# Weight decoding in a fused attention and feed-forward kernel: low parts of the first twelve blocks from TensorE instead of VectorE

## The chip, the core and the metric

The kernel runs on one core of a Trainium2 chip. A core has TensorE (PE, matrix products into PSUM), VectorE (DVE), ScalarE (ACT), GpSimd (POOL) and SyncE (SP, which here issues DMAs). Each engine takes its instructions in the order in which they were placed on it, and waits on semaphores where it needs another engine's result. The metric is the device time of one execution in microseconds (us); lower is better.

## The reference, cut to what matters

```python
B, H, S, D = 4, 8, 768, 64              # q, k, v in float32
scores = matmul(q, k.T) / 8
keep = (pos_k < n_sink) | ((0 <= pos_q - pos_k) & (pos_q - pos_k < window))   # 4 sinks, window 128
a = softmax(where(keep, scores, -1e9))
x = matmul(a, v)                        # -> 3072 rows of 512
h = x @ w_in                            # 512 x 2048
g = where(h >= 1, h, where(h <= -1, 0, (h + 1)**2 / 4))
out = g @ w_out                         # 2048 x 512
```

The weights `w_in` and `w_out` arrive as 8-byte floating-point words (the host passes the memory as pairs of 32-bit integers). The kernel turns them into float32 numbers on the chip, and then splits each into a high part (rounded to the format that TensorE reads in one pass, F32R in the code) and a low part (the rest), since each product of the feed-forward is computed as high*high + high*low + low*high.

## The kernel before, in words

The work is cut into 64 attention units of 3 blocks of 128 query rows: one head of one batch, first or second half of the sequence. Eight units (the eight heads) make a chunk of 384 rows, and there are eight chunks. Unit 0 to 7 are chunk 0, 8 to 15 chunk 1, and so on. A unit is made of: loads of q, k and v (SP); three score products (TensorE, line 239); mask and row maximum (VectorE, line 243); exponential (ScalarE, line 246); one over the sum (GpSimd line 251, VectorE line 252); normalisation (ScalarE line 264 and VectorE line 266 in the first 16 units, which are called native); transposes (TensorE lines 324 and 326), their copies out of PSUM (ScalarE lines 327 and 331); and the product with v (`av2`, line 367 for the native units) with its copy `xn` (line 369). The score products and `av2` of native units take plain float32 operands.

After a chunk's attention comes its feed-forward: `split` (lines 479, 480), 16 `stage1` steps (line 439, products with `w_i`), the activation (446 to 450) and 16 `stage2` steps (line 458, products with `w_o`). TensorE alone is written in program order by hand (`manual_schedule`): the attention steps of one chunk are interleaved with the feed-forward steps of the chunk before by `spread`. The order of all other engines is set when the program is built: a list scheduler, which runs through the program with its own estimate of each duration, places each instruction when it takes it to be ready, earlier program text first. That order is then fixed.

There are 32 weight blocks of 128 x 512 numbers, numbered n = 0 to 31: even n is block n/2 of `w_in` (tile `wi0`, `wi1`, ...), odd n of `w_out` (tile `w`). `weights(n)` loads the raw words (issued by SP for n below 8, by ScalarE after that, `AHEAD` blocks ahead) and calls `decode` (lines 151 to 157): three VectorE instructions put the float32 number together in a tile `o` (lines 153, 154, 155), ScalarE casts it to the high part (156), VectorE subtracts to get the low part (157). The tile `o` has two buffers, so that the first instruction of block n+2 (line 153) needs the last reader of block n's `o` to be done. In program order the first six blocks (`WFIRST`) are spread over the attention of units 0 to 9, when there is no feed-forward yet; the next 22 over units 10 to 17, beside the feed-forward of chunk 0's first half; the last four after that.

## Time and profile before

| | before |
|---|---|
| time, median of 3 runs | 736.66 us (735.27 to 738.84) |
| the profiled execution: its own time | 737.31 us |
| its span, first to last instruction | 735.5 us |
| TensorE busy | 696.8 us, 95% of the span |
| VectorE busy | 528.7 us, 72% |
| ScalarE busy | 507.0 us, 69% |
| GpSimd busy | 307.2 us, 42% |
| mean granted TensorE clock | 0.988 |
| DMA | 77.79 MB, mean 106 GB/s |

The shares are means over stages that differ: the first 150 us hold all weight decoding. The profile cuts the span into 40 slices of 18.4 us, and the trace can be asked for the busy time of each engine in any stretch, for the groups of instructions in it, and for the instructions in order of time. A tile's name in a row stands without its buffer number, and shapes are partitions x elements.

### The profile page before, as it was taken

What the parts mean: (1) busy time and instruction counts of PE and PEld (TensorE: products, weight loads), DVE (VectorE), ACT (ScalarE), POOL (GpSimd) and SP (SyncE); (2) the same over time, 40 slices, a digit from 0 to 9 for tenths busy, and PEclk for the clock granted to TensorE, in tenths of its full rate; (3) what the DMA queues carried; (4) which work ended last, traced back from release to release, by engine and by line L of the source; (5) the groups of instructions that cost most, each with busy time, mean ns of one, the idle gap of its engine ahead of it and who ended that gap; (6) DMA issues with size and microseconds to landing.
All of it is one profiled execution on the core that took longest, in us unless ns stands there. A gap on an engine that the chain in (4) does not pass through costs nothing.

```text
span 735.5 us, 12356 instructions
## 1 busy us (share of the span) xinstructions
PE 696.8 (95%) x3841; PEld 615.7 (84%) x3841; DVE 528.7 (72%) x1396; ACT 507.0 (69%) x1313; POOL 307.2 (42%) x537
## 2 busy tenths in 40 slices
PE   5669889899999999999999999999999999999996
PEld 3337678789999999999979998899889999989995
DVE  8999996987655666568777887877887777742221
ACT  4888797776576665578767876778767776645342
POOL 3112166554346434236554555645666454500000
PEclk9989999999999999999999999999999999999998
DMA  8987543312131311134423542324334342101001
GB/s 268 327 268 255 170 115 96 99 46 54 42 100 45 100 40 58 34 119 128 124 81 117 156 121 85 116 73 156 124 114 119 103 131 85 66 2 44 0 1 47
DMA packets 48265, 77.79 MB, mean 106 GB/s; under 512 B 13632, under 2 KB 32064, under 8 KB 48192
## 3 DMA queue, kind: packets, MB, share of 16 engines
q1 hardware_dynamic: 44736, 64.34, 28.9%
q10 hardware_dynamic: 3456, 12.58, 4.8%
q8 instruction: 32, 0.52, 0.3%
q14 instruction: 41, 0.34, 0.2%
HBM read 69.83 MB, written 7.08 MB: 105 GB/s over the span
## 4 chain that ended last, share of the span: by engine, by line
PE 64%; DVE 17%; ACT 7%; DMA 7%; issue 2%; POOL 2%; SPq 0%; ACTq 0%; POOLq 0%; DVEq 0%
PE o_ps L458 28%; PE h_ps L439 27%; PE ps_a L402 4%; DMA w<-w_in 4%; PE ps_a L239 3%; ACT p L246 2%; DVE p L266 2%; DVE k_s L223 1%; DVE o L154 1%; PE ps_a L334 1%; DVE o L155 1%; DVE p L258 1%; DVE gl L450 1%; DVE p L243 1%; DVE o L153 1%
## 5 line engine op out<-in xcount | busy, mean ns | idle before, releaser
L439 PE MATMUL h_ps<-x,wi 128*128 128x384 f32 x1536 | 308.7, 340 | 0.4 <-DVE x L480 0.4
L439 PEld LDWEIGHTS h_ps<-x,wi 128*128 128x128 f32 x1536 | 263.5, 188 | 9.3 <-DVE x L480 0.7
L458 PE MATMUL o_ps<-w,gh 128*128 128x512 f32 x768 | 244.6, 399 | 0.0
L458 PE MATMUL o_ps<-w,gl 128*128 128x512 f32 x384 | 151.3, 394 | 0.0
L458 PEld LDWEIGHTS o_ps<-w,gh 128*128 128x128 f32 x768 | 135.2, 189 | 15.7 <-issue 0.3
L446 ACT ACTIVATE g<-h_ps,half 128x384 f32<-128x384 f32 x128 | 73.9, 578 | 69.7 <-PE h_ps L439 67.7
L448 DVE SCALAR_TENSOR_TENSOR g<-g,h_ps 128x384 f32<-128x384 f32 x128 | 70.2, 549 | 68.6 <-ACT g L447 68.0
L246 ACT ACTIVATE p<-p,peak 128x260 f32<-128x260 f32 (+1 forms) x192 | 93.9, 489 | 33.9 <-DVE peak L243 32.0
L225 POOL TENSOR_TENSOR q_l<-r,q_h 128x384 fp32r<-128x384 f32 x48 | 50.3, 1047 | 142.5 <-ACT q_h L224 141.6
L449 ACT CAST gh<-g 128x384 fp32r<-128x384 f32 x128 | 65.5, 512 | 56.9 <-DVE g L448 55.9
L243 DVE CUSTOM_DVE_ANT_0 p<-ps_a,m 128x260 f32<-128x260 f32 (+1 forms) x176 | 68.5, 398 | 31.8 <-PE ps_a L239 30.5
L239 PE MATMUL ps_a<-k_s,q_h 128*128 128x260 f32 (+1 forms) x240 | 71.2, 345 | 18.6 <-DMA k_s<-qk 6.1
L458 PEld LDWEIGHTS o_ps<-w,gl 128*128 128x128 f32 x384 | 72.3, 188 | 17.5
L450 DVE TENSOR_TENSOR gl<-g,gh 128x384 fp32r<-128x384 f32 x112 | 68.0, 607 | 24.5 <-ACT gh L449 23.6
L223 DVE TENSOR_TENSOR k_s<-k_r,k_s 64x524 fp32r<-64x524 f32 (+1 forms) x44 | 45.4, 1032 | 40.9 <-ACT k_s L221 40.9
L239 PEld LDWEIGHTS ps_a<-k_s,q_h 128*128 128x128 f32 x240 | 45.2, 203 | 33.3 <-issue 10.9
L447 ACT ACTIVATE g<-g 128x384 f32<-128x384 f32 x128 | 67.0, 523 | 2.7
L346 POOL TENSOR_SCALAR_AFFINE_SELECT pt<-pt 128x384 fp32r<-128x384 f32 (+1 forms) x96 | 50.8, 530 | 24.2 <-DVE pt L339 21.7
L266 DVE TENSOR_SCALAR p<-p,stat 128x132 f32<-128x132 f32 (+1 forms) x160 | 59.1, 418 | 0.3
L344 POOL TENSOR_SCALAR_AFFINE_SELECT pt<-pt 128x384 fp32r<-128x384 f32 (+1 forms) x96 | 52.5, 547 | 8.9 <-ACT pt L338 3.9
L251 POOL TENSOR_SCALAR stat<-stat 128x3 f32<-128x3 f32 x64 | 28.6, 447 | 62.2 <-ACT p L246 53.8
L402 PEld LDWEIGHTS ps_a<-pt,v_s 128*128 128x128 f32 x304 | 46.5, 189 | 2.0
(117 smaller groups left out, 955.3 us busy)
## 6 DMA issues: line engine op xcount, KB each, us to landing
r<-qk SPq DMA_DIRECT2D x48, 192.0 KB
k_r<-qk SPq DMA_DIRECT2D x32, 262.0 KB
again<-w_in SPq DMA_DIRECT2D x16, 512.0 KB
again<-w_out SPq DMA_DIRECT2D x16, 512.0 KB
w<-w_in ACTq DMA_DIRECT2D x12, 512.0 KB
w<-w_out ACTq DMA_DIRECT2D x12, 512.0 KB
out<-o SPq DMA_DIRECT2D x23, 256.0 KB
r<-vx SPq DMA_DIRECT2D x32, 128.0 KB
```

Of the source, the lines that this page charges most:

```text
L239: nc.tensor.matmul(ps[:, lo:260], lhsT=q[:, i * P:(i + 1) * P], rhs=k_s[:, c0:c0 + 260 - lo], start=(j == 0), stop=(j == len(qs) - 1))
L243: nc.vector.tensor_tensor_reduce(out=p[:, i, lo:260], in0=ps[:, lo:260], in1=m, scale=-0.0625 if units.index(u) < NATIVE else -0.125, scal ...
L246: nc.scalar.activation(p[:, i, lo:260], p[:, i, lo:260], AF.Exp, bias=peak_i, scale=-1.0, accum_out=stat[:, i:i + 1])
L266: (nc.gpsimd if eng == "p" else nc.vector).tensor_scalar(p[:, i, lo:260], p[:, i, lo:260], r, None, op0=ALU.mult)
L402: nc.tensor.matmul(z, lhsT=w, rhs=y, start=(n == 0), stop=(n == len(mms) - 1))
L439: nc.tensor.matmul(h_ps[:, :T], lhsT=w_i[j][:, w, ct * P:(ct + 1) * P], rhs=x[:, y, ct], start=(ct == 0 and n == 0), stop=(ct == NCT - 1 a ...
L446: nc.scalar.activation(g, h_ps[:, :T], AF.Relu, bias=half, scale=0.5)
L447: nc.scalar.activation(g, g, AF.Square)
L448: nc.vector.scalar_tensor_tensor(g, g, 1.0, h_ps[:, :T], op0=ALU.min, op1=ALU.max)
L449: nc.scalar.copy(gh, g)
L450: (nc.gpsimd if row0 == GL_POOL else nc.vector).tensor_tensor(gl, g, gh.bitcast(F32), op=ALU.subtract)
L458: nc.tensor.matmul(o_ps[tt], lhsT=gg[:, tt * P:(tt + 1) * P], rhs=w_o[j][:, w], start=(j == js[0] and n == 0), stop=(j == js[-1] and n == 2))
```

## The change

For blocks 0 to 11 the subtraction on VectorE is left out. Two matrix products take its place: identity times the float32 number `o` (plain float32 operands), and minus identity times the high part (F32R operands), added up in one PSUM tile of the pool `ps_o`; ScalarE copies this out into the low part. `weights(n)` calls this (`lows`) for block n-1 after it has decoded block n. `neg` is minus the identity. `WFIRST` goes from 6 to 12, so that blocks 0 to 11 are spread over units 0 to 9, and blocks 12 to 27 over units 10 to 17. Blocks 12 to 31 are decoded as before, the subtraction now on line 158. All lines behind it have numbers that are 19 higher than before (243 becomes 262, 324 becomes 343).

```diff
-WFIRST = 6
+WFIRST = 12
...
-    def decode(t, w, words):
+    def decode(t, w, words, lo=True):
         low, x = words[:, :, 0], words[:, :, 1]
         nc.vector.tensor_scalar(w, x, 3, 0x3FFFFFFF, op0=ALU.logical_shift_left, op1=ALU.bitwise_and)
         nc.vector.scalar_tensor_tensor(w, x, -0x40000000, w, op0=ALU.bitwise_and, op1=ALU.bitwise_or)
         nc.vector.scalar_tensor_tensor(w, low, 29, w, op0=ALU.logical_shift_right, op1=ALU.bitwise_or)
         nc.scalar.copy(t[:, 0], w.bitcast(F32))
-        nc.vector.tensor_tensor(t[:, 1], w.bitcast(F32), t[:, 0].bitcast(F32), op=ALU.subtract)
+        if lo:
+            nc.vector.tensor_tensor(t[:, 1], w.bitcast(F32), t[:, 0].bitcast(F32), op=ALU.subtract)
+
+
+    neg = const.tile([P, P], F32R, name="neg")
+    nc.vector.tensor_scalar(neg, ident, -1.0, None, op0=ALU.mult)
+    todo = {}
+
+    def lows(n):
+        if n not in todo:
+            return
+        t, w = todo.pop(n)
+        ps = ps_o.tile([P, DM], F32, name="o_ps")
+        nc.tensor.matmul(ps, lhsT=ident, rhs=w.bitcast(F32), start=True, stop=False)
+        nc.tensor.matmul(ps, lhsT=neg, rhs=t[:, 0], start=False, stop=True)
+        nc.scalar.copy(t[:, 1], ps)
...
-            decode((w_i, w_o)[i][j], moe.tile([P, DM], I32, name="o"), words)
+            t, w = (w_i, w_o)[i][j], moe.tile([P, DM], I32, name="o")
+            decode(t, w, words, n >= WFIRST)
+            lows(n - 1)
+            if n < WFIRST:
+                todo[n] = t, w
```

How this moves instructions shows best at three places. The first is VectorE where unit 10 begins, the first unit that runs beside the feed-forward. `p_651` (before) and `p_736` (changed) are the score tile of unit 10, `o_...` the number of a block, `wi8` the low and high part of block 16, `wi6` that of block 12. Before:

```order
L157 TENSOR_TENSOR w_1006<-o_1007,w_1006 128x512
L154 SCALAR_TENSOR_TENSOR o_1022<-w_915,o_1022 128x512
L153 TENSOR_SCALAR o_1057<-w_968 128x512
L155 SCALAR_TENSOR_TENSOR o_1022<-w_915,o_1022 128x512
L154 SCALAR_TENSOR_TENSOR o_1057<-w_968,o_1057 128x512
L243 ISA p_651,peak_97<-ps_a_653,m0_109 128x128
L243 ISA peak_97 128x1
L243 ISA p_651,peak_97<-ps_a_665,m1n_108 128x260
L243 ISA peak_97 128x1
L155 SCALAR_TENSOR_TENSOR o_1057<-w_968,o_1057 128x512
L157 TENSOR_TENSOR wi8_159<-o_1022,wi8_159 128x512
```

And with the change:

```order
L153 TENSOR_SCALAR o_744<-w_610 128x512
L271 RECIPROCAL stat_678<-stat_678 128x3
L154 SCALAR_TENSOR_TENSOR o_744<-w_610,o_744 128x512
L285 TENSOR_SCALAR p_677<-p_677,stat_678 128x128
L155 SCALAR_TENSOR_TENSOR o_744<-w_610,o_744 128x512
L262 ISA p_736,peak_97<-ps_a_738,m0_109 128x128
L262 ISA peak_97 128x1
L153 TENSOR_SCALAR o_805<-w_653 128x512
L158 TENSOR_TENSOR wi6_157<-o_744,wi6_157 128x512
```

Before, unit 10 begins on VectorE when blocks 0 to 15 are done and two more are begun: ahead of it stand 18 instructions of line 153, 18 of line 154, 17 of line 155 and 16 of line 157. With the change, 13 of each of lines 153 to 155 stand ahead of it and no subtraction; block 12 is the newest.

The second place is TensorE, program order, from unit 3's scores (`ps_a_317` before, `ps_a_332` now) on. Before:

```order
L239 MATMUL ps_a_317<-k_s_263,q_h_262 128x128
L239 MATMUL ps_a_321<-k_s_263,q_h_262 128x260
L239 MATMUL ps_a_325<-k_s_263,q_h_262 128x260
L324 MATMUL ps_a_334<-ident_79,p_268 128x128 x2
L326 MATMUL ps_a_334<-ident_79,p_268 4x128
L324 MATMUL ps_a_341<-ident_79,p_268 128x128 x3
L367 MATMUL ps_a_346<-pt_251,v_s_227 64x128 x2
L367 MATMUL ps_a_346<-pt_251,v_s_227 64x256 x4
```

With the change, where `o_302` is the number of block 2, `o_352` that of block 3:

```order
L258 MATMUL ps_a_340<-k_s_276,q_h_275 128x260
L170 MATMUL o_ps_357<-o_302,ident_79 128x512
L171 MATMUL o_ps_357<-wi1_152,neg_169 128x512
L343 MATMUL ps_a_361<-ident_79,p_281 128x128 x2
L345 MATMUL ps_a_361<-ident_79,p_281 4x128
L343 MATMUL ps_a_368<-ident_79,p_281 128x128 x3
L386 MATMUL ps_a_373<-pt_264,v_s_228 64x128 x2
L386 MATMUL ps_a_373<-pt_264,v_s_228 64x256 x4
L386 MATMUL ps_a_373<-spn0_143,v_s_228 64x128
L386 MATMUL ps_a_373<-spn1_144,v_s_228 64x128
L170 MATMUL o_ps_390<-o_352,ident_79 128x512
L171 MATMUL o_ps_390<-w_351,neg_169 128x512
```

The pair of products for block n stands between a unit's scores and the transposes of the unit before, or behind `av2`. It needs ScalarE's cast of block n, and everything behind it on TensorE waits with it.

The third place is VectorE where the 29th block (block 28, `wi14`) is finished. Before, that is ahead of unit 16 (`p_1233`), and 28 rows later unit 18 begins:

```order
L157 TENSOR_TENSOR w_1434<-o_1435,w_1434 128x512
L448 SCALAR_TENSOR_TENSOR g_1167<-g_1167,h_ps_1125 128x384
L157 TENSOR_TENSOR wi14_165<-o_1472,wi14_165 128x512
L243 ISA p_1233,peak_97<-ps_a_1235,m0_109 128x128
L243 ISA peak_97 128x1
```

With the change it is right ahead of unit 18 (`p_1503`):

```order
L360 TENSOR_TENSOR sk1_133<-ps_a_1400,sk1_133 8x128
L499 TENSOR_TENSOR x_1482<-xn_171,x_1482 128x384
L155 SCALAR_TENSOR_TENSOR o_1510<-w_1415,o_1510 128x512
L158 TENSOR_TENSOR wi14_165<-o_1510,wi14_165 128x512
L467 SCALAR_TENSOR_TENSOR g_1456<-g_1456,h_ps_1437 128x384
L262 ISA p_1503,peak_97<-ps_a_1505,m0_109 128x128
```

So by unit 18 both programs have put the same work behind them on VectorE, except for the 12 subtractions that are gone. Between unit 10 and unit 18 the changed program has 16 instructions of each of lines 153, 154 and 155 and 17 subtractions, where there were 11, 11, 12 and 13.

## The prediction

> **What bounds the kernel now.** I read the page's summary first, then the busy time of each engine in stretches cut at two events that both programs have: VectorE's first score instruction of unit 10 (60.6 us) and of unit 18 (117.7 us). I call what lies before the first stage A, between them stage B.
>
> ```profile
> PE 696.8 (95%) x3841; PEld 615.7 (84%) x3841; DVE 528.7 (72%) x1396; ACT 507.0 (69%) x1313; POOL 307.2 (42%) x537
> PE   5669889899999999999999999999999999999996
> DVE  8999996987655666568777887877887777742221
> ```
>
> ```profile
> core 0: us, PE busy (x) PEld busy (x) DVE busy (x) ACT busy (x) POOL busy (x), PEclk, DMA share, GB/s
> 0.00:60.60 60.60, 41.69 (x187) 24.67 (x188) 56.59 (x176) 44.67 (x134) 10.99 (x47) 0.92 0.86 286
> 60.60:104.90 44.30, 39.72 (x229) 32.02 (x228) 43.14 (x106) 37.58 (x107) 14.54 (x17) 0.96 0.57 178
> 104.90:117.70 12.80, 12.13 (x77) 10.25 (x77) 9.63 (x31) 10.48 (x32) 9.95 (x14) 1.00 0.29 87
> 117.70:160.00 42.30, 38.73 (x220) 34.33 (x220) 35.98 (x98) 30.22 (x84) 21.82 (x38) 1.00 0.30 86
> 160.00:700.00 540.00, 535.34 (x2992) 488.64 (x2992) 376.16 (x977) 372.28 (x939) 249.87 (x421) 1.00 0.29 87
> ```
>
> Over the span TensorE is the bound, but not in the first slices. In stage A VectorE is busy 56.6 of 60.6 us and TensorE 41.7; up to 104.9 VectorE has 43.1 of 44.3. From 160 us on TensorE has 535 of 540. So the end comes as late as the early stages let TensorE begin its full run: a microsecond won or lost by unit 18 reaches the end, because behind it TensorE idles only 3.6 us up to 160 (work that the change does not touch) and then next to nothing, and nothing there can catch up.
>
> **What VectorE does in the two stages.** Groups of its instructions by shape, stage A, then stage B:
>
> ```profile
> L154 DVE SCALAR_TENSOR_TENSOR o<-w,o 128x512 int32<-128x512 int32 x18 | 12.3, 683 | 0.1
> L155 DVE SCALAR_TENSOR_TENSOR o<-w,o 128x512 int32<-128x512 int32 x17 | 11.6, 682 | 0.0
> L153 DVE TENSOR_SCALAR o<-w 128x512 int32<-128x512 int32 x18 | 7.5, 419 | 0.5 <-DVE stat L252 0.3 <-DMA w<-w_in 0.2
> L157 DVE TENSOR_TENSOR w<-o,w 128x512 fp32r<-128x512 f32 x8 | 5.5, 682 | 0.0
> L157 DVE TENSOR_TENSOR wi<-o,wi 128x512 fp32r<-128x512 f32 x8 | 5.4, 680 | 0.0
> ```
>
> ```profile
> L155 DVE SCALAR_TENSOR_TENSOR o<-w,o 128x512 int32<-128x512 int32 x12 | 9.8, 820 | 0.0
> L154 DVE SCALAR_TENSOR_TENSOR o<-w,o 128x512 int32<-128x512 int32 x12 | 9.4, 786 | 0.1
> L157 DVE TENSOR_TENSOR wi<-o,wi 128x512 fp32r<-128x512 f32 x7 | 5.6, 806 | 0.0
> L153 DVE TENSOR_SCALAR o<-w 128x512 int32<-128x512 int32 x11 | 5.4, 490 | 0.1
> L157 DVE TENSOR_TENSOR w<-o,w 128x512 fp32r<-128x512 f32 x6 | 4.5, 754 | 0.9 <-ACT w L156 0.9
> ```
>
> Before, 18 blocks are begun in stage A, although program order asks for only six there: VectorE fills every gap with decoding. The same instructions are dearer in stage B (820 against 682 ns) where GpSimd is busier. In order of time, at the end of stage A and at unit 18:
>
> ```profile
> 57.85 0.68 DVE L157 TENSOR_TENSOR w<-o,w 128x512 fp32r<-128x512 f32 x1
> 58.45 0.68 DVE L154 SCALAR_TENSOR_TENSOR o<-w,o 128x512 int32<-128x512 int32 x1
> 59.06 0.42 DVE L153 TENSOR_SCALAR o<-w 128x512 int32<-128x512 int32 x1
> 59.39 0.68 DVE L155 SCALAR_TENSOR_TENSOR o<-w,o 128x512 int32<-128x512 int32 x1
> 59.99 0.68 DVE L154 SCALAR_TENSOR_TENSOR o<-w,o 128x512 int32<-128x512 int32 x1
> 60.60 0.28 DVE L243 CUSTOM_DVE_ANT_0 p<-ps_a,m 128x128 f32<-128x128 f32 x1
> 117.71 0.29 DVE L243 CUSTOM_DVE_ANT_0 p<-ps_a,m 128x128 f32<-128x128 f32 x1 [0.46 <-PE ps_a L239]
> ```
>
> Durations overlap, so what one instruction costs is start to start: 0.60 us for line 157 (57.85 to 58.45), 0.61 for 154, 0.33 for 153, 0.60 for 155. A block is 2.14 us, without its subtraction 1.54.
>
> **The change, term 1: VectorE in stage A.** By the orders shown it loses 16 of line 157 (9.6 us), 5 of 153 (1.7), 5 of 154 (3.0) and 4 of 155 (2.4): 16.7 us. By VectorE alone unit 10 could begin at 60.6 - 16.7 = 43.9. The one instruction for `neg` lies in VectorE's first wait and costs nothing (0.3 us if not).
>
> **Term 2: ScalarE in stage A.** It gets 11 copies out of PSUM and loses 4 casts. The copy of the same shape out of the same pool, the first activation of the kernel, ScalarE's longest wait in stage A, and a cast with a weight load issued inside it:
>
> ```profile
> 124.60 0.57 ACT L464 COPY o<-o_ps 128x512 f32<-128x512 f32 x1
> 7.61 0.40 ACT L246 ACTIVATE p<-p,peak 128x128 f32<-128x128 f32 x1 [5.54 <-DVE peak L243]
> ACT p L246 <- DVE peak L243: 10.2, 9, 5.5
> 56.52 0.61 ACT L156 CAST w<-o 128x512 fp32r<-128x512 f32 x1
> 56.60 0.42 ACTq L167 DMA_DIRECT2D w<-w_in  x1
> ```
>
> 11 x 0.57 - 4 x 0.61 = +3.8 us. ScalarE was busy 44.7 us; 1.3 of that is a table load ahead of 7.6 us, so it needs at least 7.6 + 43.4 + 3.8 = 54.8 us. In its order it begins unit 10 about 3 us behind VectorE (five or six of its instructions at 0.4 to 0.6 us stand between), so VectorE's unit 10 comes at 51.8 at the earliest. Above that come waits. Before, ScalarE idled 60.6 - 7.6 - 43.4 = 9.6 us behind its start, about half of it for VectorE's score instructions (10.2 less the first 5.5). VectorE is quicker now, but TensorE's products, and ScalarE's copies behind them, are new waits. From 0 to 9.6 us of idle time, unit 10 comes at 51.8 to 61.4. I take 4.7 us, half: **56.5**. The gain of stage A is then 4 us, not 16.7: ScalarE takes the place of VectorE.
>
> The weight loads that ScalarE issues move with their blocks (13 before unit 10, now 9). Each lies beside an activation, as at 56.60, so I put them at nothing; without that cover 4 x 0.42 = 1.7 us, gained in A and lost in B.
>
> **Term 3: TensorE.** No plain float32 product of 512 columns is in the trace. The nearest rows are the native scores (two records for one product) and `stage2`:
>
> ```profile
> 73.13 0.60 PE L239 MATMUL ps_a<-k_s,q_h 128*128 128x260 f32 x2
> 73.38 0.81 PE L458 MATMUL o_ps<-w,gh 128*128 128x512 f32 x2
> 197.20 0.63 PE L458 MATMUL o_ps<-w,gh 128*128 128x512 f32 x2
> 197.89 0.62 PE L458 MATMUL o_ps<-w,gh 128*128 128x512 f32 x2
> ```
>
> Three F32R products of 512 columns take 0.69 us (197.20 to 197.89), 0.23 each; a float32 product of 260 columns takes 0.25 for two records, so one of 512 columns takes 0.46 to 0.49. A block costs 0.69 to 0.72 us, 11 of them 7.9 us in stage A, where TensorE idles 60.6 - 41.7 = 18.9. It fits, so as work it costs nothing; if that cover were gone, 7.9 us. As a wait it counts: behind each pair stand the transposes, `av2` and the next unit's scores, for which ScalarE's copies and VectorE wait, and line 153 of block n+2 waits for the first product of block n, which reads `o`. That is in the 4.7 us of idle.
>
> The Trainium skill says more against this change: in "FP8 and Floating Point Precision", section TensorE Precision Notes, true FP32 takes four passes through the array. By it a block would cost 5 x 0.23 = 1.15 us, an estimate, and TensorE 12.7 us. The rows at 73.13 and 73.38 show two passes and decide.
>
> **Term 4: VectorE in stage B.** What A leaves comes here: 5 more of line 153, 5 of 154, 4 of 155, 4 of 157. At stage A's start to start 1.7 + 3.0 + 2.4 + 2.4 = 9.5 us; with what stage B's means are higher by (71, 103, 138 and about 101 ns, together 1.8) 11.3. Stage B was 57.1 us: 52.8 busy (43.14 + 9.63) and 4.3 idle. It becomes 52.8 + 9.5 = 62.3 if no idle is left, and 52.8 + 11.3 + 4.3 = 68.4 if all of it stays. Most of the idle time lay behind 104.9, where no decoding was left to fill it; now decoding goes on until unit 18. I take 10.4 and half of the idle: **65.4**. TensorE (51.9 busy) and ScalarE (48.1 + 4 x 0.61 + 0.57 = 51.1) stay below that.
>
> **Sum.** Unit 18 at 56.5 + 65.4 = 121.9 us, against 117.7: +4.2. From there the programs do the same work. The profiled execution took 737.3 us (span 735.5 and 1.8 around it): 741.5, forecast 741.5. The median before was 736.66, 0.65 below the profiled run; by that 740.9, a difference that the range covers. The twelve subtractions (12 x 0.60 = 7.2 us) do leave VectorE, but in the stage where something else becomes the bound, and four to five blocks are pushed to where it is still the bound.
>
> **Rivals.**
> - *Faster.* ScalarE runs stage A without a wait and VectorE stage B without a gap: 51.8 + 62.3 = 114.1, -3.6, 733.7. With VectorE as the only bound throughout, 117.7 - 7.2 - 4.3 = 106.2 would be 726, but ScalarE's 54.8 us stand against it. It decides from unit 10 before 51.6 on (117.7 - 3.7 - 62.4), below ScalarE's bound of 51.8 unless its lag behind VectorE grows. Chance 0.16.
> - *No change.* Unit 10 at 54.0 and stage B at 64: 118.0, 737.6. For it: TensorE's gaps in stage A are filled, so its clock may stay up, and the same `av2` pair (its first twelve records) varied with it:
>
> ```profile
> 32.28 1.30 PE L367 MATMUL ps_a<-pt,v_s 128*64 128x128 f32 x12
> 44.89 2.11 PE L367 MATMUL ps_a<-pt,v_s 128*64 128x128 f32 x12
> ```
>
>  Two such pairs less stretched are 1.6 us; the granted clock was 0.92 over stage A. The Trainium skill ("TensorE: Matmul & The Clock Gate", Part 1) has sustained activity release the clock, which no run here shows for the added products. Chance 0.36.
> - *Slower by far.* The added products are as slow as four passes, or the waits of TensorE and ScalarE on each other keep all 9.6 us of idle: unit 10 at 61.4, stage B at 66: 127.4, 747. Chance 0.12.
> - *The change does not do what it says*: blocks 0 to 11 not earlier, but fewer in stage A. The orders say so already; it is a part of the forecast.
>
> **How the numbers follow.** The forecast (unit 18 at 121.5 to 125.5, 741 to 745) has 0.36. About 0.5% (3.7 us) is what a measurement of this kernel can tell from no change. Slower by more: 0.36 + 0.12 = 0.48; within it: 0.36; faster: 0.16. The range for 8 in 10 goes from 733, just below the faster rival, to 750, above the slow one (51.8 to 61.4 and 62.3 to 68.4 would give 733.7 to 749.4).
>
> **What would show it.** In the changed profile VectorE's busy share up to unit 10 falls to about 40 of 56 us, and ScalarE's rises to 48; ScalarE waits there for TensorE's `o_ps`. Unit 10 begins at 52 to 61 us, unit 18 at 119 to 126, VectorE is busy without gaps between them, and the stage behind is as long as before. The added products take 0.69 to 0.72 us for a pair. I am wrong if unit 10 comes before 51 us, if stage B takes less than 62, or if the time behind unit 18 changes by more than 2 us.

## The result, and the profile after

The changed kernel takes 745.55 us (median of 4 runs, 744.15 to 746.45) beside 735.96 us for the kernel before on the same chip (4 runs): a ratio of 1.0123, 95% interval 1.0096 to 1.0150. It is slower by 9.6 us, about twice what was forecast (+4.2). The profiled execution took 745.4 us, with a span of 743.6 against 735.5, so +8.1. First the page of the changed kernel, the busy times and two rows of the 40 slices:

```profile
PE 706.7 (95%) x3877; PEld 623.4 (84%) x3877; DVE 523.9 (70%) x1385; ACT 511.0 (69%) x1325; POOL 309.7 (42%) x537
PE   6889969899999999999999999999999999999996
DVE  7679998897754666657787788768878777842221
```

VectorE has become lighter (523.9 us against 528.7). In the sixth slice (93 to 112 us) TensorE has a 6 where it had an 8, and in the seventh VectorE has an 8 where it had a 6. The loss has to be sought there. I cut the first 158 us at the first score instruction of units 10, 16, 18 and 21 on VectorE. Before and after (columns: window, length, then the busy time of PE, PEld, DVE, ACT and POOL with counts, the granted clock, DMA share and GB/s):

```profile
0.00:60.60 60.60, 41.69 (x187) 24.67 (x188) 56.59 (x176) 44.67 (x134) 10.99 (x47) 0.92 0.86 286
60.60:104.86 44.26, 39.68 (x229) 31.98 (x228) 43.10 (x105) 37.54 (x107) 14.54 (x17) 0.96 0.57 178
104.86:117.71 12.85, 12.18 (x77) 10.30 (x78) 9.67 (x31) 10.53 (x32) 9.95 (x14) 1.00 0.29 88
117.71:149.64 31.93, 28.36 (x161) 24.96 (x160) 27.78 (x72) 22.00 (x61) 17.15 (x29) 1.00 0.33 96
```

```profile
0.00:57.65 57.65, 45.32 (x214) 28.26 (x215) 42.32 (x147) 46.39 (x140) 9.91 (x47) 0.97 0.79 256
57.65:101.69 44.04, 41.27 (x241) 32.97 (x239) 42.91 (x105) 37.60 (x109) 14.74 (x17) 1.00 0.64 208
101.69:124.86 23.17, 16.11 (x82) 12.60 (x83) 22.08 (x48) 12.90 (x36) 13.95 (x15) 0.85 0.31 99
124.86:158.02 33.16, 29.19 (x151) 25.75 (x149) 27.86 (x72) 21.89 (x60) 16.38 (x28) 0.90 0.31 95
```

Stage A (up to unit 10) became 2.95 us shorter, and units 10 to 15 run as fast as before (44.0 against 44.3), so that unit 16 begins 3.2 us earlier. Then the two units 16 and 17 take 23.17 us instead of 12.85. Nearly all of the loss lies here: 10.3 us lost, less the 3.2 won before it, is the 7.15 us by which unit 18 is late. Another 1.2 us goes by unit 21, and behind unit 21 both have the same time to go (585.9 us before, 585.6 after).

In these 23.17 us VectorE is busy all the time (22.08) and TensorE is not (16.11). What VectorE does there (start, length, what), and what TensorE waits for:

```profile
101.69 0.29 DVE L262 CUSTOM_DVE_ANT_0 p<-ps_a,m 128x128 f32<-128x128 f32 x1
...
105.92 1.50 DVE L155 SCALAR_TENSOR_TENSOR o<-w,o 128x512 int32<-128x512 int32 x1
...
107.56 0.42 DVE L153 TENSOR_SCALAR o<-w 128x512 int32<-128x512 int32 x1
...
108.93 0.68 DVE L154 SCALAR_TENSOR_TENSOR o<-w,o 128x512 int32<-128x512 int32 x1
...
109.62 0.99 DVE L158 TENSOR_TENSOR w<-o,w 128x512 fp32r<-128x512 f32 x1
110.53 0.68 DVE L155 SCALAR_TENSOR_TENSOR o<-w,o 128x512 int32<-128x512 int32 x1
111.13 1.43 DVE L285 TENSOR_SCALAR p<-p,stat 128x128 f32<-128x128 f32 x3
```

```profile
106.01 0.40 PE L477 MATMUL o_ps<-w,gl 128*128 128x512 f32 x1
112.22 0.94 PE L353 MATMUL ps_a<-ident,p 128*128 128x128 f32 x3 [5.81 <-DVE p L285]
```

Line 285 is the normalisation of unit 16, all of it on VectorE from this unit on; TensorE transposes the result (line 353) and has nothing else to do in its order. Between unit 16's scores and this normalisation VectorE has eight instructions of weight decoding in its order (lines 153, 154, 155, 158), and the normalisation comes 9.4 us behind the first score (101.69 to 111.13) instead of 4.4 (104.86 to 109.27 before, with no decoding between them). TensorE stands still for 5.8 us. The row of the kernel before:

```profile
109.27 0.68 DVE L266 TENSOR_SCALAR p<-p,stat 128x128 f32<-128x128 f32 x3
```

From unit 16's first score to unit 18's there are 17 decoding instructions; before, there was none: by unit 16 all 29 blocks had been decoded. With the change only 25 blocks had been begun by then.

The added pairs on TensorE, between a transpose and the next work of its order:

```profile
49.44 0.27 PE L345 MATMUL ps_a<-ident,p 128*4 128x128 f32 x1
49.55 1.02 PE L170 MATMUL o_ps<-o,ident 128*128 128x512 f32 x2
50.01 0.81 PE L171 MATMUL o_ps<-w,neg 128*128 128x512 f32 x1
50.65 0.49 PE L343 MATMUL ps_a<-ident,p 128*128 128x128 f32 x3
```

From the pair's start to the next start is 1.10 us (49.55 to 50.65), not 0.69 to 0.72.

### The profile page after: what moved, and what is told of

Read it like the earlier page. It is cut to its first block, busy times and chain, and to the rows that moved or that the text cites. A ratio compares the mean times of both kernels' runs of the same rounds, so it can differ in the third digit from the quotient of the medians.

```text
span 743.6 us, 12440 instructions
## 1 busy us (share of the span) xinstructions
PE 706.7 (95%) x3877; PEld 623.4 (84%) x3877; DVE 523.9 (70%) x1385; ACT 511.0 (69%) x1325; POOL 309.7 (42%) x537
## 4 chain that ended last, share of the span: by engine, by line
PE 63%; DVE 15%; ACT 11%; DMA 5%; issue 4%; POOL 3%; ACTq 0%; SPq 0%; POOLq 0%; DVEq 0%
PE o_ps L477 26%; PE h_ps L458 26%; PE ps_a L421 4%; ACT p L265 3%; PE ps_a L258 3%; DMA r<-qk 2%; DVE p L285 2%; DVE k_s L242 1%; PE ps_a L353 1%; DVE gl L469 1%; DVE p L277 1%; ACT p L283 1%; DVE g L467 1%; ACT k_s L240 1%; DVE pt L358 1%
## 5 line engine op out<-in xcount | busy, mean ns | idle before, releaser
L469 DVE TENSOR_TENSOR gl<-g,gh 128x384 fp32r<-128x384 f32 x112 | 65.5, 585 | 25.2 <-ACT gh L468 24.5
L258 PE MATMUL ps_a<-k_s,q_h 128*128 128x260 f32 (+1 forms) x240 | 67.4, 327 | 12.4 <-DMA k_s<-qk 4.9
L242 DVE TENSOR_TENSOR k_s<-k_r,k_s 64x524 fp32r<-64x524 f32 (+1 forms) x44 | 45.9, 1044 | 44.3 <-ACT k_s L240 44.2
L365 POOL TENSOR_SCALAR_AFFINE_SELECT pt<-pt 128x384 fp32r<-128x384 f32 (+1 forms) x96 | 50.8, 529 | 28.1 <-DVE pt L358 24.4
```

The costliest lines, as they stand in the source:

```text
L258: nc.tensor.matmul(ps[:, lo:260], lhsT=q[:, i * P:(i + 1) * P], rhs=k_s[:, c0:c0 + 260 - lo], start=(j == 0), stop=(j == len(qs) - 1))
L469: (nc.gpsimd if row0 == GL_POOL else nc.vector).tensor_tensor(gl, g, gh.bitcast(F32), op=ALU.subtract)
```

## The experiments

The question was why so much decoding is left at unit 16. **Theory 1**, the prediction's: fewer blocks are decoded by unit 10, because ScalarE is the bound of stage A and the two buffers of `o` tie VectorE to TensorE. **Rivals**: the number 12 (`WFIRST`) alone moves the decoding; ScalarE's copies; TensorE's time for the twelve products, wherever they stand. The table has all experiments; "begun" counts the blocks whose first instruction (line 153) stands ahead of unit 10 in VectorE's order, "left" the decoding instructions in the trace between unit 16's first score and unit 18's; times in us, spans of the profiled execution. "(one)" is the time of a single run.

| run | begun | unit 10 | unit 16 | left | unit 18 | span | median |
|---|---|---|---|---|---|---|---|
| before | 18 | 60.6 | 104.9 | 0 | 117.7 | 735.5 | 735.96 |
| the change | 13 | 57.7 | 101.7 | 17 | 124.9 | 743.6 | 745.55 |
| number 12 alone | 20 | 65.5 | 108.1 | 0 | 122.0 | 741.6 | 743.32 (one) |
| change, six `o` buffers | 23 | 69.6 | 108.6 | 0 | 122.8 | 741.3 | 742.40 |
| change, less for ScalarE | 13 | 58.4 | 102.1 | 17 | 124.5 | 743.2 | 744.95 (one) |
| change, products swapped | 13 | 57.6 | 103.3 | 14 | 125.7 | 744.9 | 746.58 (one) |
| before + ten product pairs | 18 | 59.5 | 105.3 | 0 | 118.9 | 736.3 | 739.65 |
| change, no products, no copy | 20 | 63.7 | 103.6 | 0 | 117.5 | 736.0 | 737.86 |
| GpSimd subtracts | 16 | 63.4 | 108.0 | 5 | 125.3 | 741.3 | 744.44 |
| change, six blocks, number 6 | 8 | 50.8 | 98.7 | 24 | 124.5 | 741.2 | 744.48 |
| change, no copy | 13 | 60.0 | 103.7 | 17 | 126.1 | 743.8 | 745.46 |
| no products, no copy, number 6 | 20 | 62.0 | 102.7 | 0 | 115.4 | 733.4 | 736.55 |
| change, steps set earlier | 17 | 59.9 | 103.8 | 1 | 117.1 | 736.1 | 738.20 |
| change, three blocks, number 6 | 14 | 58.4 | 102.7 | 12 | 124.8 | 740.9 | 742.26 |

The kernel before had medians of 734.83, 736.75 and 736.27 us beside the first four experiments, the next four and the last four; each ratio below is against the one of its own set.

### The number 12 alone

```diff
-WFIRST = 6
+WFIRST = 12
```

> Only the number of blocks that are spread over units 0 to 9 goes from 6 to 12; all low parts stay with VectorE. Theory (the loss comes from tying VectorE to TensorE through the two buffers of o, which leaves only 13 blocks ahead of unit 10): the number alone costs nothing, because VectorE filled its gaps with decoding anyway. Its order now has 20 blocks ahead of unit 10 and 29 ahead of unit 18, so unit 10 on VectorE moves from 60.6 us to about 65 (two more blocks of 2.14 us), unit 18 stays at 117 to 119 us, and the time at 735 to 739 us. Rival (the new spread itself pushes the units back): unit 18 at 122 us or later, 741 us or more.

Measured: 743.32 us in one run, beside 734.83; span +6.1. The theory was right about the order (20 blocks, unit 10 at 65.5) and wrong about unit 18 and the time, for which the rival's figures hold, unit 18 (121.97) just at its edge.

```profile
0.00:65.50 65.50, 41.22 (x186) 25.53 (x187) 61.25 (x183) 46.43 (x136) 11.85 (x47) 0.90 0.83 279
65.50:108.09 42.59, 38.99 (x225) 31.53 (x224) 38.15 (x98) 37.00 (x106) 12.27 (x18) 0.96 0.52 170
108.09:121.97 13.88, 12.96 (x82) 11.01 (x82) 9.13 (x31) 9.71 (x29) 9.88 (x14) 1.00 0.21 59
```

Asking for twelve blocks ahead of unit 10 costs, by this one run, nearly as much as the whole change, but in another place: 20 blocks are begun in stage A instead of 18, VectorE is busy 61.25 of 65.5 us there, and unit 10 comes 4.9 us late. Units 16 and 17 take 13.9 us; nothing is left to decode. The decoding that was brought forward is not paid back: VectorE has only 38.15 of 42.59 us in the next stage, and TensorE, with 39 of 42.6, doesn't let it become much shorter. So decoding too early and decoding too late both cost; the change pays the second.

### Six buffers for `o`

```diff
+    six = []
...
+            if n < WFIRST and not six:
+                six.append(xpool.tile([P, 6, DM], I32, name="x"))
-            t, w = (w_i, w_o)[i][j], moe.tile([P, DM], I32, name="o")
+            t, w = (w_i, w_o)[i][j], six[0][:, n % 6] if n < WFIRST else moe.tile([P, DM], I32, name="o")
```

> The changed kernel, with six buffers instead of two for the numbers o of blocks 0 to 11 (in memory that is idle at that time), so that line 153 of block n+2 no longer waits for TensorE's product of block n. In its order 22 blocks stand ahead of unit 10, where the changed kernel has 13. Theory (the tie through o is the cause): VectorE is busy again for at least 53 of the 60 us of stage A, unit 18 comes at 108 to 115 us instead of 124.9, and the time is 727 to 735 us, faster than before the change. Rival (the added ScalarE copies and TensorE products cost the time themselves): unit 10 at 64 us or later, unit 18 at 119 us or later, 738 us or more.

Measured: 742.40 us, ratio 1.0088 (1.0064 to 1.0112). The theory of that time was wrong about the time and right about the tie. The rival's three figures all hold, but its reason is not needed for them: the number 12 alone, without products and copies, gave a span within 0.3 us of this one. With six buffers the tie is gone: 23 blocks are begun by unit 10 and none is left at unit 16. But now stage A is 69.6 us long, and as with the number 12 alone the later units can't use it:

```profile
0.00:69.60 69.60, 49.12 (x216) 29.56 (x216) 60.85 (x183) 51.41 (x150) 10.86 (x47) 0.95 0.82 279
69.60:108.60 39.00, 38.11 (x231) 31.69 (x230) 30.55 (x87) 35.88 (x104) 12.51 (x18) 1.00 0.53 158
```

From 69.6 to 108.6 us TensorE is busy 38.1 of 39.0 us; VectorE, with 30.6, is no bound any more.

### Less work for ScalarE, and no copy

```diff
-            eng = NORM[i] if units.index(u) < NATIVE else "v"
+            eng = ("vva" if units.index(u) < 10 else NORM)[i] if units.index(u) < NATIVE else "v"
```

> The changed kernel; in units 0 to 9 one of the two normalisations that ScalarE does (0.50 us each, 10 in all) goes to VectorE, which idles 15 of 57.7 us in stage A of the changed kernel. Theory (the tie through o): the same 13 blocks stand ahead of unit 10, so at most the units themselves get quicker: unit 10 at 55 to 58 us instead of 57.65, unit 18 at 122 to 125, 743 to 746 us. Rival (ScalarE's 46.4 us are the bound of stage A): unit 10 at 53 us, unit 18 at 120, 741 us.

```diff
-        nc.scalar.copy(t[:, 1], ps)
+        nc.gpsimd.memset(t[:, 1].bitcast(F32), 0.0)
```

> The changed kernel with its product pairs, but without ScalarE's copy: the low parts of blocks 0 to 11 are set to zero by GpSimd (left out of the computation). Theory now (the first product of a pair, at its place in TensorE's order, holds the o buffer and so VectorE's next block; ScalarE's copies are beside the point): unit 10 within 1.5 us of 57.65, stage B 65 us or more, 742 to 745 us. Rival (ScalarE is what bounds stage A, as the prediction had it; it loses 12 x 0.57 = 6.8 us): unit 10 at 52 to 55, 738 to 741 us.

These ask whether ScalarE bounds stage A, as term 2 of the prediction had it. Stage A of the two runs, ScalarE's busy time the fourth of the five:

```profile
0.00:58.40 58.40, 45.89 (x214) 29.22 (x215) 44.76 (x157) 43.26 (x131) 10.38 (x47) 0.97 0.80 260
```

```profile
0.00:60.03 60.03, 46.00 (x214) 28.62 (x215) 45.39 (x146) 41.84 (x130) 15.03 (x59) 0.97 0.77 246
```

ScalarE lost 3.1 and 4.6 us of its 46.4, and unit 10 came later, not earlier: 58.4 and 60.0 against 57.65, both above the theory's ranges. The times stayed: 744.95 us (one run), and 745.46 us without the copy against 745.55 with it, 0.5 us above the theory's range. Neither run is a clean test. In the first VectorE takes over what ScalarE lost (44.76 us busy against 42.32). In the second the stage begins late: of GpSimd's memsets, which stand in for the low parts, five run together at the very start; beside them one small VectorE instruction takes 2.18 us (0.16 in the changed kernel), and the first score comes at 9.78 us instead of 7.31. All three runs with such memsets show this. The rows are those of the last of them, with no products, no copy and the number 6 (further down); its lines 82 and 260 are 81 and 262 in the run without the copy:

```profile
5.24 2.38 POOL L170 MEMSET wi<- 128x512 f32 x5
5.46 2.18 DVE L82 TENSOR_SCALAR big<-par_f 128x2 f32<-128x2 f32 x1
9.78 0.29 DVE L260 CUSTOM_DVE_ANT_0 p<-ps_a,m 128x128 f32<-128x128 f32 x1
```

Counted from the first score, unit 10 comes at 50.3 us both with the copy and without it. So ScalarE's copies cost stage A nothing; what their absence brings later, up to these 2.5 us, may be hidden in the time. And ScalarE alone does not set the length of stage A, although it has the largest part of the chain of work that ends last there: in the changed kernel, by my sum over the chain's pieces up to 57.65 us, ScalarE has 30.3 of 57.0 us, VectorE 11.0 and TensorE 8.0. The chain's largest parts by line:

```profile
by line: ACT p L265 18.3%; ACT p L283 10.6%; issue 8.7%; ACT pt L346 6.2%; PE o_ps L170 4.8%; ACT wi L156 3.8%; ACT w L156 3.8%; ACT wi L172 3.8%; PE ps_a L343 3.4%; DVE par_f L74 3.3%; DMA par_i<-par 2.9%; DVE o L153 2.7%; DVE o L154 2.6%;
```

Without the copy ScalarE has 11.9 us of that chain, TensorE 24.7 and VectorE 18.5, and the stage is no shorter: other chains of about the same length lie beside it.

### The two products swapped

```diff
-        nc.tensor.matmul(ps, lhsT=ident, rhs=w.bitcast(F32), start=True, stop=False)
-        nc.tensor.matmul(ps, lhsT=neg, rhs=t[:, 0], start=False, stop=True)
+        nc.tensor.matmul(ps, lhsT=neg, rhs=t[:, 0], start=True, stop=False)
+        nc.tensor.matmul(ps, lhsT=ident, rhs=w.bitcast(F32), start=False, stop=True)
```

> The changed kernel with the two products of a pair in the other order: minus identity times the high part first, then the float32 product. It tells which of the two takes the long time behind it: in the changed kernel the second record of a pair comes 0.23 us after the first, the F32R product 0.23 us after that, and the next instruction 0.63 us later. If the float32 product takes four passes (its two records begin early, the array is held longer), the float32 records now follow the F32R product after 0.21 to 0.25 us and the next instruction on TensorE begins 0.6 us or more after the second of them. If the F32R product is slow by itself, the 0.63 us now stand behind it, ahead of the first float32 record. Time within 2 us of the changed kernel in both cases (743 to 748 us).

Here line 170 is the F32R product and line 171 the plain float32 one:

```profile
49.30 0.48 PE L170 MATMUL o_ps<-w,neg 128*128 128x512 f32 x1
49.62 1.02 PE L171 MATMUL o_ps<-o,ident 128*128 128x512 f32 x2
50.48 0.49 PE L343 MATMUL ps_a<-ident,p 128*128 128x128 f32 x3
```

The float32 product takes 0.86 us (49.62 to 50.48) wherever it stands: in the changed kernel 0.46 us show between its start and the next product's, and the rest behind that one, which seems to take 0.64. Against 0.23 us for an F32R product of the same size that is nearly four times as much. The Trainium skill ("FP8 and Floating Point Precision", TensorE Precision Notes) has true FP32 take four passes through the array, and the trace agrees: 4 x 0.23 = 0.92, an estimate, against 0.86. The time, 746.58 us (one run), is within the 2 us of the change's that were expected: the order of the two makes no difference that this run can show.

### The products alone

```diff
+    neg = const.tile([P, P], F32R, name="neg")
+    nc.vector.tensor_scalar(neg, ident, -1.0, None, op0=ALU.mult)
...
             decode((w_i, w_o)[i][j], moe.tile([P, DM], I32, name="o"), words)
+            for _ in range(2 if 0 < n < WFIRST else 0):
+                ps = ps_o.tile([P, DM], F32, name="o_ps")
+                nc.tensor.matmul(ps, lhsT=ident, rhs=w_i[0][:, 1].bitcast(F32), start=True, stop=False)
+                nc.tensor.matmul(ps, lhsT=neg, rhs=w_i[0][:, 0], start=False, stop=True)
```

> The kernel before, with ten product pairs added on TensorE (two beside each of blocks 1 to 5, from the finished low and high part of block 0, result not used); VectorE and ScalarE do what they did before. Theory now (TensorE's time is the price: a pair takes 1.09 us, and part of the 10.9 us stands ahead of products that ScalarE and VectorE wait for): unit 10 at 63 to 67 us instead of 60.6, 738 to 743 us. Rival (the pairs lie in TensorE's 18.9 us of idle time in stage A and cost nothing): unit 10 within 1 us of 60.6, 735 to 737 us.

Measured: 739.65 us, ratio 1.0042 (1.0029 to 1.0055): +3.1 us. Neither side was right: the time lies in the theory's range, unit 10 does not. Ten pairs, 11 us of TensorE, are mostly hidden, but not free: unit 10 came even earlier (59.46, with a granted clock of 1.00 over stage A instead of 0.92), unit 18 1.2 us later. At this price twelve are 3.7 us, an estimate, and not the change's +9.6. Their operands lay ready, so this is the price of TensorE's time alone, without waits for ScalarE's cast.

### Neither products nor copy, with the numbers 12 and 6

```diff
-        ps = ps_o.tile([P, DM], F32, name="o_ps")
-        nc.tensor.matmul(ps, lhsT=ident, rhs=w.bitcast(F32), start=True, stop=False)
-        nc.tensor.matmul(ps, lhsT=neg, rhs=t[:, 0], start=False, stop=True)
-        nc.scalar.copy(t[:, 1], ps)
+        nc.gpsimd.memset(t[:, 1].bitcast(F32), 0.0)
```

> The changed kernel without the product pairs and without ScalarE's copy: the low parts of blocks 0 to 11 are set to zero by GpSimd (they are left out of the computation). VectorE keeps its relief of twelve subtractions, the number of blocks ahead of unit 10 stays 12. Theory now (products and copies are what the relief is paid with; the number 12 alone costs 6 us of span): 7.2 us less than with the number 12 alone, 733 to 737 us, unit 10 at 57 to 60, unit 18 at 114 to 118. Rival (VectorE's subtractions do not set the pace of the first 120 us; waits between attention's engines do): 740 us or more, unit 18 at 120 or later.

> The kernel without subtraction, products and copy for blocks 0 to 11 (their low parts are set to zero by GpSimd and so left out of the computation), as in the run without products and copy, but with the number 6 as before the change: what the idea could bring at the very best. Theory now (the two effects add up: the number 12 costs 6 us, the relief of VectorE brings 5.6): 729 to 732 us. Rival (without subtractions VectorE isn't the bound any more, so that the number no longer matters): 734 to 738 us.

For the second run the blocks without subtraction stay 0 to 11 and `WFIRST` is 6. Measured: 737.86 us (1.0025, interval 1.0008 to 1.0043) and 736.55 us (1.0000, interval 0.9973 to 1.0028). The first missed its range by 0.9 us, and its unit 10 (63.7) by 3.7. The second is the surprise, and its rival was right: with hardly any work for the low parts the kernel is not measured faster than before. The two effects do not add up: the two runs are 1.3 us apart, where the theory had 6.

```profile
0.00:62.03 62.03, 39.56 (x185) 25.48 (x186) 57.91 (x174) 46.39 (x137) 17.24 (x59) 0.92 0.89 295
62.03:102.67 40.64, 37.95 (x230) 31.14 (x229) 34.58 (x95) 36.27 (x105) 14.28 (x18) 1.00 0.57 178
```

VectorE fills the time of the twelve subtractions with further blocks (20 by unit 10 instead of 18; 57.9 us busy), so stage A doesn't shrink (62.0 us, 59.5 without its late start); and in the next stage, where VectorE has room (34.6 of 40.6), TensorE has 37.95 of 40.64 us. So 7.2 us less on VectorE, its busiest stage included, were worth at most 0.3% of the whole in this measurement. Its late start of 2.5 us comes with the memsets and not with the idea; how much of it reaches the end no run shows. If all of it did, the relief would be worth up to 2.0 + 2.5 = 4.5 us, an estimate, still less than the 7.2. The profile shown is that of an execution of 735.09 us, faster than the median; its unit 18 (115.4 against 117.7) therefore says little. I had read VectorE's 56.6 of 60.6 us as a bound, but part of it was decoding that nobody waited for yet.

### GpSimd subtracts

```diff
-    def decode(t, w, words):
+    def decode(t, w, words, n=99):
...
-        nc.vector.tensor_tensor(t[:, 1], w.bitcast(F32), t[:, 0].bitcast(F32), op=ALU.subtract)
+        (nc.gpsimd if n < 12 else nc.vector).tensor_tensor(t[:, 1], w.bitcast(F32), t[:, 0].bitcast(F32), op=ALU.subtract)
...
-            decode((w_i, w_o)[i][j], moe.tile([P, DM], I32, name="o"), words)
+            decode((w_i, w_o)[i][j], moe.tile([P, DM], I32, name="o"), words, n)
```

> The kernel before, with the subtractions of blocks 0 to 11 on GpSimd instead of VectorE; no products, no copy, number of blocks ahead as before (6). Theory now (VectorE's time in the first 120 us counts, and the other engine has to have room): GpSimd is busy 11 of the first 60 us and gets 12 x about 1.5 = 18 us; VectorE loses 7.2 us and its other instructions become dearer by up to 6 us: 730 to 737 us. Rival (the buffers of o are held longer by the slower reader, and hold up VectorE as in the changed kernel): 738 to 743 us, with 16 blocks or fewer begun by unit 10 and waits of line 153 for GpSimd.

Measured: 744.44 us, ratio 1.0117 (1.0093 to 1.0142). The time lies above both ranges, on the rival's side, and the 16 blocks begun are the rival's too, but the waits that it named are not there: in stage A no line 153 waits for GpSimd. VectorE's instructions became dearer, by more than I had put down. Stage A of this run:

```profile
L155 DVE SCALAR_TENSOR_TENSOR o<-w,o 128x512 int32<-128x512 int32 x16 | 13.7, 854 | 0.0
L154 DVE SCALAR_TENSOR_TENSOR o<-w,o 128x512 int32<-128x512 int32 x16 | 12.6, 786 | 0.1
L153 DVE TENSOR_SCALAR o<-w 128x512 int32<-128x512 int32 x16 | 9.1, 568 | 0.4 <-DMA w<-w_in 0.4
L157 POOL TENSOR_TENSOR w<-o,w 128x512 fp32r<-128x512 f32 x6 | 8.4, 1405 | 1.0 <-ACT w L156 1.0
```

854, 786 and 568 ns against 682, 683 and 419 before: 172 + 103 + 149 = 424 ns a block, 6.8 us for 16 blocks, about what the subtractions would have brought. Two blocks fewer are begun by unit 10, and five decoding instructions are left at unit 16. The dearer instructions can't be the reason for that, because the order is fixed before the kernel runs. That the scheduler takes `o` to be held longer by GpSimd, which is the rival's reason at another place, would explain it; this was not tested.

### Half the change, with the number 6

```diff
-WFIRST = 12
+WFIRST = 6
```

> The changed kernel with the number 6 in place of 12: products and copies for blocks 0 to 5 only, six blocks asked for ahead of unit 10 as before. Theory now (two o buffers tie VectorE's next block to the place of the products in TensorE's order, six places up to unit 10): only 8 blocks stand ahead of unit 10, which comes early, at 46 to 54 us, stage B has 19 blocks and takes 70 us or more, unit 18 at 121 to 127, 739 to 745 us. Rival (the number 12 is what costs, products and copies cost nothing): unit 18 at 114 to 118, 732 to 736 us.

Measured: 744.48 us, ratio 1.0122 (1.0095 to 1.0148), unit 10 at 50.75 us, stage B 73.7, unit 18 at 124.48: the theory's numbers. Six products, spread over units 0 to 9 in TensorE's order, let VectorE begin no more than 8 blocks there. Its shape is that of the change, only more so:

```profile
0.00:50.75 50.75, 39.57 (x198) 24.79 (x198) 34.98 (x131) 40.29 (x129) 9.62 (x47) 1.00 0.76 237
...
98.73:124.48 25.75, 17.68 (x83) 13.03 (x83) 25.69 (x55) 14.28 (x39) 14.26 (x16) 0.80 0.43 140
```

Stage A is 9.9 us shorter than before, and units 16 and 17 take 25.75 us, all of them VectorE's (25.69).

### Three blocks, with the number 6

```diff
-WFIRST = 12
+WFIRST = 6
+LOWN = 3
...
-            decode(t, w, words, n >= WFIRST)
+            decode(t, w, words, n >= LOWN)
...
-            if n < WFIRST:
+            if n < LOWN:
```

> The changed kernel with products and copies for blocks 0 to 2 only, and the number 6 as before. Theory now (each block whose product has its place in TensorE's order delays VectorE's decoding, and three of them give 1.8 us of relief): 14 blocks stand ahead of unit 10 instead of 18, which are decoded in stage B: unit 18 at 118 to 122, 736 to 741 us. Rival (the gain comes first and the ties only with later blocks): unit 18 at 115 to 117, 733 to 735 us.

Measured: 742.26 us, ratio 1.0079 (1.0049 to 1.0109); 14 blocks by unit 10, twelve decoding instructions left at unit 16, unit 18 at 124.76: on the theory's side and somewhat above both of its ranges. Three tied blocks out of 32 are enough.

### The same twelve steps, set earlier in TensorE's order

```diff
-        for _, f in spread(attn, prev, LEAD if c else 1.0):
+        for _, f in spread(attn, prev, LEAD if c else 2.0):
```

> The changed kernel with its twelve weight steps set twice as early among the attention steps of units 0 to 9 in TensorE's order (a factor of 2 in place of 1 where they are interleaved), nothing else changed. Theory now (the place of the products in TensorE's order sets how many blocks VectorE gets done by unit 10): 17 blocks instead of 13 stand ahead of unit 10, unit 10 at 58 to 63, stage B 57 to 61, unit 18 at 117 to 122, 736 to 741 us. Rival (the price is TensorE's time for twelve pairs, wherever they stand): unit 18 at 124 or later, 743 us or more.

Measured: 738.20 us, ratio 1.0019 (0.9999 to 1.0040), with all twelve products and copies done as in the change, and all of the theory's figures held. Products, copies and the number are those of the change; only the place of the twelve steps among the attention steps differs, and of its +9.6 us over the kernel before 1.9 are left:

```profile
0.00:59.87 59.87, 44.94 (x214) 28.07 (x215) 50.77 (x163) 48.28 (x144) 10.07 (x47) 0.98 0.86 287
59.87:103.83 43.96, 41.77 (x241) 33.01 (x240) 42.88 (x106) 37.86 (x107) 13.63 (x17) 0.99 0.57 179
103.83:117.07 13.24, 11.70 (x72) 9.59 (x73) 9.22 (x33) 10.90 (x33) 9.86 (x14) 1.00 0.33 93
```

In stage A VectorE is busy 50.8 us instead of 42.3, 17 blocks are begun instead of 13, one decoding instruction is left at unit 16, and units 16 and 17 take 13.2 us. So most of the loss comes from the place of the steps, and about 1.9 us of it, up to 2.9 by the interval, from all else that the change adds. A step is a load, a decoding and a product pair, and all of it moved: that it is the products' place in TensorE's hand-written order, which sets when `o` is free and so how many blocks VectorE gets done, follows from this run together with others. With the change's products left out 20 blocks are begun, at the number 12 as at 6, and with six buffers 23; with the products there and two buffers it is 8 (six steps over units 0 to 9), 13 (twelve) or 17 (twelve, set earlier). No run was faster than the kernel before.

Over the table, units 16 and 17 take 12.7 to 14.2 us where at most one decoding instruction is left, 17.3 where five are, and 22 to 26 where twelve or more are.

## Why the prediction was right, and where not

**Forecast and direction.** Slower was right, and 745.55 lies in the range, but the forecast of 741.5 was too low, and 745.55 is just above the 741 to 745 for which it stood. By the spans, +8.1 against +4.2; the 3.9 us between them are 1.15 at unit 10 (57.65, not 56.5), 1.8 in stage B (67.2 us, not 65.4), and 0.95 behind unit 18.

**"Four to five blocks are pushed to where it is still the bound"** (VectorE) was right, and is the cause. Steps set earlier take it away; half the change has more of it (24 instructions left, 25.75 us for units 16 and 17). What the prediction did not have is the place: not all of stage B, but the two units at its end, whose normalisation is all on VectorE and stands behind the decoding. Up to unit 16 nothing was lost.

**Term 1 and the tie to TensorE.** That VectorE alone could have begun unit 10 at 43.9 was a bound that no run with 17 or more blocks came near. The run without products and copy, number 6, has unit 10 at 62.0, or 59.5 without its late start. Freed time is filled with more blocks.

**Term 2** gave a good number with a good deal of luck. "ScalarE takes the place of VectorE" is only in part so: ScalarE has just over half of the chain that ends last in stage A, but with 3.1 and 4.6 us less for it unit 10 did not come earlier. Two sizes missed in opposite directions: ScalarE's busy time up to unit 10 rose by 1.7 us (44.67 to 46.39), not by 3.8, and ScalarE began unit 10 at 58.61 us, 0.96 behind VectorE, not 3. The idle time fits (57.65 - 7.6 - 45.1 = 5.0 us behind ScalarE's start, where I took 4.7). The longest waits of VectorE in stage A:

```profile
DVE o L153 <- PE o_ps L170: 5.0, 3, 3.5
DVE stat L271 <- POOL stat L270: 1.7, 4, 0.6
```

Columns here: the sum in us, how many, the longest. Line 153 waits 5.0 us for the product that reads `o`; the prediction named this wait and left it in a lump of idle time. It is the smaller part of the tie: the larger one is that the order already puts five blocks fewer there.

**Term 3** failed. "0.69 to 0.72 us" for a pair measured 1.10 us, and the claim that the rows at 73.13 and 73.38 "show two passes and decide" was a misreading. The 0.25 us between those starts is not what the float32 product took; its time shows behind the start of the next one, as in the swapped products. The next row of that trace says so:

```profile
74.03 0.40 PE L458 MATMUL o_ps<-w,gl 128*128 128x512 f32 x1
```

The two F32R products begun at 73.38 take until 74.03, 0.65 us instead of 0.46. With these 0.19 us the float32 product of 260 columns took 0.44, near the 0.47 that four passes of 260 columns would take (4 x 260/512 x 0.23, an estimate). The Trainium skill's four passes, which I set aside, are the rule that holds. The price was small: ten pairs alone cost 3.1 us, and what twelve cost beyond that comes from their place, not from their time.

**Term 4** had the stage too short by 1.8 us but inside its bounds (62.3 to 68.4). VectorE was busy 64.99 of 67.21 us, without gaps as forecast, and the idle time is the 2.2 us that I took. The added busy time was mis-sized: 64.99 - 52.8 = 12.2 us, where I took 10.4 and had 11.3 as the most. Decoding was not dearer than in stage B before: by the means of its instructions a block takes 2.88 us in both. The normalisation was, which term 4 left as it stood (before, then changed):

```profile
L266 DVE TENSOR_SCALAR p<-p,stat 128x128 f32<-128x128 f32 x8 | 3.8, 469 | 0.2
L266 DVE TENSOR_SCALAR p<-p,stat 128x132 f32<-128x132 f32 x4 | 1.1, 320 | 0.0
L285 DVE TENSOR_SCALAR p<-p,stat 128x128 f32<-128x128 f32 x8 | 5.5, 689 | 0.0
L285 DVE TENSOR_SCALAR p<-p,stat 128x132 f32<-128x132 f32 x4 | 1.9, 509 | 0.0
```

That is 2.5 us more for the same twelve instructions. Within the stage, decoding is dearest where it stands in units 16 and 17 (line 155: 990 ns a piece there, 739 up to unit 16). One row shows how: line 155 took 1.50 us at 105.92 (the row is shown above), with GpSimd busy from 105.53 to 106.88:

```profile
105.53 1.35 POOL L242 TENSOR_TENSOR k_s<-k_r,k_s 64x392 fp32r<-64x392 f32 x1
```

Its undisturbed length is 0.68 us; it ended at 107.42, 0.54 behind GpSimd's end. The Trainium skill ("SBUF — State Buffer", Who interferes with whom) has a VectorE instruction with two SBUF inputs contend with a GpSimd instruction that reads SBUF; this row agrees.

**Behind unit 18** the time changed by 0.95 us, within the 2 us that I allowed, and the way there is not quite nothing: units 18 to 20 took 33.2 us instead of 31.9. In the other runs they took between 30.6 and 34.3 us, the ones without any added work among the longest, so it is not the added work. What it is was not tested and stays open.

**The rivals.** Faster: fell; no run is measured faster than the kernel before, and even with the late start allowed for, the run with hardly any work for the low parts stays far from the 726 us of "VectorE as the only bound throughout". No change: its reason, the clock, came true in stage A (0.97 instead of 0.92), but unit 10 came at 57.65 and not at 54.0, and stage B took 67.2 us and not 64; with its steps set earlier the change comes near this rival's time. Slower by far (747): its first half, four passes, was true, and its second, that the waits keep all idle time, was not; the time came near it by another way.

## What to carry to other kernels

An engine that is busy nearly all of a stage need not be its bound: some of the work may be early work that fills gaps, and taking work off such an engine may do little more than let it run further ahead. When work moves to an engine whose order is written by hand, its place in that order sets when the buffer that it reads comes free, and so how far the engine that fills the buffer can run ahead: look for the first place where the delayed work stands ahead of something on the critical path (here the first unit normalised on VectorE alone), and set the moved step early enough for that. When a run leaves work out, see in its trace what the stand-in does: here three runs with memsets began 2.5 us late. And take the cost of a matrix product from starts of the same kind of work on both sides of it, not from its own record or the very next one.

## What the runs showed of the hardware

A plain float32 product of 512 columns takes 0.86 us, against 0.23 for an F32R one, while its two records start early and let the following product seem slow (0.64 us). Twelve GpSimd subtractions of 128x512 (1.3 to 1.4 us each) made VectorE's decoding instructions on the same stage 103 to 172 ns dearer, 6.8 us over 16 blocks against the 7.2 us that the subtractions took there. In all three runs with five GpSimd memsets in a row near the start, one 128x2 VectorE instruction beside them took 2.18 us instead of 0.16. When TensorE waited in units 16 and 17, the granted clock over them was 0.85 instead of 1.00; it was 0.77 to 0.85 in the six kernels with twelve or more decoding instructions left there.
